# Attention kernel for one core: projections in column tiles and halves, VectorE work without the shared port, an early key tile, another output order

## Chip, cores and metric

One core of one Trainium2 chip. The metric is the device time of one execution in microseconds (us).

Engine names as the profile has them: PE is TensorE, PEld its weight load, ACT is ScalarE, DVE is VectorE, POOL is GpSimd, SP issues most DMAs. A line such as L1701 is a line of the kernel in question, so the same operation has other line numbers in other kernels.

## The reference, cut to what matters

```python
# S = 2048, D = 512, H = 32 heads of 16
def _A_ref(x, wq, wk, wv, wo):              # one key and value head for all query heads
    q = (x @ wq).reshape(B, S, H, 16).transpose(0, 2, 1, 3)
    k, v = x @ wk, x @ wv
    p = softmax(einsum("bhqd,bkd->bhqk", q, k) * 0.25)
    return heads_joined(einsum("bhqk,bkd->bhqd", p, v)) @ wo
def _B_ref(x, wqkv, w_phi, wo):             # linear attention
    q, k, v = ...                           # x @ wqkv
    pq, pk = q @ w_phi, k @ w_phi           # per head
    phi = lambda t: concat([softmax(t), softmax(-t)])
    kv, z = phi(pk)^T @ v, sum(phi(pk))
    return heads_joined((phi(pq) @ kv) / (phi(pq) @ z + 1e-6)) @ wo
return concat([_A_ref(...), _B_ref(...)], axis=-1)
```

Part A needs 32 x 2048 x 2048 exponentials, 2048 score tiles of 128x512. Part B is small.

## The kernel before

Half of the work is a Python list scheduler that runs while the program is built. Each piece of work is a job with an engine, an estimated length, predecessors and a priority; the scheduler keeps a model clock for every engine, and its order becomes the fixed order of each engine's instructions. A score tile's exponential goes to ACT (two tiles to one instruction, `f_PT`) or to DVE, which makes the bits of the result as an int16 (`f_Z`); POOL then shifts the bits of four such tiles at a time, three times, by integer additions, and each of the four versions has its own value product. Which tiles go where is decided as the model clock runs, so **any edit moves the split between ACT and DVE**.

```python
LOCK = ("dS", "qw")        # DVE jobs that must not run beside a POOL instruction
NEAR = 0.15                # us: a POOL addition due this soon goes ahead of such a job
T_B = (54.0, 600.0)        # when part B is released

def run(self):             # one round of the list scheduler
    ...
            t = max(r, self.pe_from(j, te) if eng == "pe" else te)
            j.asked = t
            if eng == "pool" or j.name[0] in self.LOCK:
                t = max(t, self.te_port)        # the port that DVE and POOL share is free
    ...
    s, j = min(picks, key=lambda p: (p[0], p[1].asked))
    if j.eng == "dve" and j.name[0] in self.LOCK:
        s, j = next((p for p in picks if p[1].eng == "pool" and p[1].asked <= s + self.NEAR
                     and self.te_port <= s + self.NEAR), (s, j))
    ...
def issue(self, j, start):
    ...
    if j.eng == "pool" or j.name[0] in self.LOCK:
        self.te_port = start + dur

def b_projv(self, st):     # one of six projections: four full-array matmuls in one piece
    for dc in range(4):
        mm = pe.matmul(ps[:, bank, :], lhsT=xT[:, dc, st*128:(st+1)*128], rhs=w[:, dc, :],
                       start=(dc == 0), stop=(dc == 3))
def b_bm(self, st):        # running sum of the softmax sums, 16 times
    v.tensor_tensor(out=bmx, in0=ssum[:, r, :], in1=bmx, op=ALU.add)
def b_vr(self, st):        # reciprocal, cast to bf16, 16 times
    v.tensor_copy(out=self.vS[:, r, :, :, 16:17], in_=rs.unsqueeze(3))

def finish_last(self):     # the tail: last denominator, then four output tiles of part A
    for i in (2, 3, 0, 1):
        ...                # products whose terms are there; 2 and 3 take all of them here
    for h in range(2):     # halves of the last denominator, shuffled to all partitions
        v.stream_shuffle(lnd[:, c], ps[:, ACC, c], [16] * 32)
    ...                    # 1/x = exp(-ln x) on ACT, multiplication, last products
    for i in (2, 0, 3, 1):
        eng = "act" if i > 1 else "dve"         # 0 and 1 add a partial product made before
        ...
        q.dma_start(out[0, (12+i)*128:(13+i)*128, 0:512], oa[:, i, :])   # queue: act if i > 1 else sp
```

Of the kernel before, what the change touches and what calls it, by code (L numbers as in the profile page):

```python
# [1160 lines left out]
class _Fast:  # L1161
# [15 lines left out]
    def __init__(self, nc, st, ins, out):  # L1177
# [24 lines left out]
        self.bmx = sb("bmx", [128, 64], F32)  # L1202
# [20 lines left out]
        self.ssum = sb("ssum", [128, 2, 64], F32)  # L1223
# [18 lines left out]
        self.free = [4, 5, 6, 7]  # L1242
        self.rec = None
# [10 lines left out]
        self.beside = False  # L1254
# [33 lines left out]
    def job(self, name, eng, dur, fn, after=(), mode=None, nb=0, frees=(), rel=0.0, prio=5.0, ok=None):  # L1288
        j = _Job(name, eng, dur, fn, after, mode, nb, frees, rel, prio, ok)
        j.left = {a for a in j.left if a not in self.issued}  # L1290
        self.njobs += 1
        j.seq = self.njobs
        for a in j.left:
            self.waiting.setdefault(a, []).append(j)
        if not j.left:
            self.cand[eng].append(j)
        return j

    def ready(self, j):
# [6 lines left out]
        t = j.rel  # L1306
# [11 lines left out]
        if nb:  # L1318
            fr = sorted(max(self.tr.get(("PS", b), (0.0,))[0], 0.0) + self.SEM for b in self.free)
            if len(fr) < nb:  # L1320
                return None
            t = max(t, fr[nb - 1])
        return t

    def issue(self, j, start):
# [11 lines left out]
        if j.eng == "pe":  # L1337
            self.beside = j.name[0] == "dq"
# [5 lines left out]
        if j.nb:  # L1344
            bs = sorted(self.free, key=lambda b: (self.tr.get(("PS", b), (0.0,))[0], b))[:j.nb]
            for b in bs:
                self.free.remove(b)
            self.bk[j.name] = bs
            self.held += j.name[0] != "dq"
        acc = self.acc_of(j)  # L1350
        if acc:
            self.bk[acc] = [min(self.free, key=lambda b: (self.tr.get(("PS", b), (0.0,))[0], b))]
# [75 lines left out]
    def head(self):  # L1428
# [27 lines left out]
        add("pool", lambda g: g.memset(self.bmx, 0.0), writes=["bmx"])  # L1456
# [31 lines left out]
        for k, t in (("wk_rep", 2.0), ("half1", 1.0), ("wv", 6.5), (("wq", 0), 3.5), (("wq", 1), 6.0), ("VA1", 3.0), ("ones", 1.0), ("zero", 1.0), ("bmx", 14.0), (("step", 0), 8.0), (("step", 1), 8.0)):  # L1488
            self.tw[k] = (t, "sp")
# [10 lines left out]
    def jobs_a(self):  # L1500
        ps, xT, job = self.ps, self.xT, self.job
        for kc in range(4):
            u = 0 if kc == 0 else 2
            job(("pk", kc), "pe", 0.86, (lambda kc: (lambda: self.proj_k(kc)))(kc), mode="full", nb=1, prio=u)
# [3 lines left out]
            job(("aK", kc), "dve", 0.60, (lambda kc: (lambda: self.absmax(self.KR[:, 0, kc * 512:kc * 512 + 512], kc, [("KR", 0, kc)])))(kc), after=[("KR", 0, kc)] + [("qa", 0)] * (kc == 0), prio=6)  # L1508
            job(("pva", kc), "pe", 0.42, (lambda kc: (lambda: self.proj_va(kc)))(kc), after=[("pq", 0), ("pk", kc)], mode="full", nb=1, prio=u + 0.5)
            job(("va", kc), "dve", 0.65, (lambda kc: (lambda: self.proj_va2(kc)))(kc), after=[("pva", kc)], frees=[("pva", kc)], prio=u + 0.5)  # L1510
        for ch in range(16):
            job(("pq", ch), "pe", 0.86, (lambda ch: (lambda: self.proj_q(ch)))(ch), mode="full", nb=1, prio=0 if ch == 0 else 2.2,
                ok=(lambda ch: (lambda: ch < 1 or (self.asc >= 2 * ch - 3 and (ch < 3 or self.qleft[2 * ch - 6] + self.qleft[2 * ch - 5] == 0))))(ch),
                after=[("pq", ch - 1)] if ch else [])
            job(("qa", ch), "dve", 0.60, (lambda ch: (lambda: self.proj_q2(ch)))(ch), after=[("pq", ch)], frees=[("pq", ch)], prio=1)
            job(("aq", ch), "dve", 0.60, (lambda ch: (lambda: self.absmax(self.QA[:, ch % 3, :], 4 + ch, [("QA", ch % 3)])))(ch), after=[("qa", ch)], prio=6)
        for qt in range(12):
            job(("op", qt), "pe", 0.86, (lambda qt: (lambda: self.outproj(qt)))(qt), mode="full", nb=1, prio=3.0, after=[("on", qt // 4 * 8 + a) for a in range(8)])
# [10 lines left out]
    def proj_k(self, kc):  # L1529
        ps, xT = self.ps, self.xT  # L1530
        bank = self.bank(("pk", kc))

        def fn(pe):
            mm = None
            for dc in range(4):
                mm = pe.matmul(ps[:, bank, :], lhsT=self.wk_rep[:, dc, :], rhs=xT[:, dc, kc * 512:(kc + 1) * 512], start=(dc == 0), stop=(dc == 3))
            return mm
        self.add("pe", fn, reads=[("AxT", kc), "wk_rep"], writes=[("PS", bank)])

    def proj_k2(self, kc, e):  # L1540

        ps, bank, half = self.ps, self.bank(("pk", kc)), self.half
        dst = self.KR[:, e, kc * 512:(kc + 1) * 512]
        self.add("dve", lambda v: v.tensor_scalar(out=dst, in0=ps[:, bank, :], scalar1=half[:, e:e + 1], scalar2=None, op0=ALU.mult),
                 reads=[("PS", bank), "half1"] + [("half", g) for g in range(4)], writes=[("KR", e, kc)])

# [26 lines left out]
    def proj_q(self, ch):  # L1573
# [3 lines left out]
        bank = self.bank(("pq", ch))  # L1577

        def fn(pe):
            mm = None  # L1580
            for dc in range(4):
                mm = pe.matmul(ps[:, bank, :], lhsT=self.wq[:, dc, A * 128:A * 128 + 128], rhs=xT[:, dc, qc * 512:(qc + 1) * 512], start=(dc == 0), stop=(dc == 3))  # L1582
            return mm
        self.add("pe", fn, reads=[("AxT", qc), ("wq", min(A, 1))], writes=[("PS", bank)])

    def proj_q2(self, ch):
        self.copy(self.QA[:, ch % 3, :], self.ps[:, self.bank(("pq", ch)), :], [("PS", self.bank(("pq", ch)))], [("QA", ch % 3)])
# [21 lines left out]
    def next_qk(self, i):  # L1609
# [6 lines left out]
        if not us:  # L1616
# [4 lines left out]
        self.job(("qk", i), "pe", 0.218, lambda: self.qk(us, b0), mode="row", prio=0, after=[("qa", sc // 2) for sc in {u[0] for u in us}] +  # L1621
                 [("KR", sc, k) for sc, k in {(u[0] % 2, u[1] // 4) for u in us}] + ([("qk", i - 1)] if i else []))
# [5 lines left out]
    def qk(self, us, b0):  # L1628
        reads = set()
        for sc, kap, g in us:  # L1630
            reads |= {("QA", sc // 2 % 3), ("KR", sc % 2, kap // 4)}
# [76 lines left out]
    def dq_ok(self):  # L1708
        if self.dbusy > self.DBUSY or self.dz_out >= self.NOUT:
            return False  # L1710
        if self.mode != "row" or self.beside:
# [777 lines left out]
```

## Time and profile before

| | before |
|---|---|
| time, median of 3 runs | 713.73 us (712.76 to 714.05) |
| span of the profiled run | 711.0 us |
| ACT exponentials / DVE tiles | 700 / 648 |
| head, ACT's stretch, tail | 9.25, 685.9, 15.8 us |

The output multiplications of part A on DVE, by line (shortest, median and longest in ns, then the start of the first and the last):

```profile
L1879 DVE TENSOR_TENSOR f_On<-f_accS,f_denS x16: 677/912/1375, 53.8 to 696.0; 128x512 bf16<-128x512 f32 x16
L1879 DVE TENSOR_TENSOR f_Ot<-f_accS,f_denS x15: 681/693/1207, 74.1 to 674.0; 128x512 bf16<-128x512 f32 x15
```

Both inputs lie in SBUF, and the same work takes 0.68 or 1.4 us. POOL's additions, from the costliest groups (busy us, mean ns, idle time before them and what ended it):

```profile
L1782 POOL INT64_ADD f_Z<-f_Z x486 | 512.7, 1055 | 167.5 <-DVE f_Z L1752 128.1
```

POOL is busy for 512.7 of 711.0 us. Of the 31 multiplications 16 take over 0.75 us, and each of these 16 overlaps a POOL instruction in the trace; 12 of the other 15 overlap one too and are not stretched. And the end of the tail, from the timeline (start, us, engine, line):

```profile
700.56 0.44 DVE L1942 STREAM_SHUFFLE f_ET<-f_ps 128x256 f32<-128x256 f32 x1
...
703.74 0.97 SPq L1961 DMA_DIRECT2D out_dram<-f_outA  x2
704.22 0.39 ACTq L1961 DMA_DIRECT2D out_dram<-f_outA  x1
...
705.29 1.12 ACTq L1961 DMA_DIRECT2D out_dram<-f_outA  x1
```

The four output tiles are issued between 703.74 and 705.29 and land, by the trace's DMA records, at 707.20, 707.51, 707.84 and 708.14. Then 2.9 us of fixed ending follow.

### The profile page before, as it was taken

Reading aid. Unit: us, or ns where it says so; the run is one execution under the profiler, and the core shown is the slowest. Engines: PE = TensorE matmul, PEld = TensorE weight load, DVE = VectorE, ACT = ScalarE, POOL = GpSimd, SP = SyncE. Lnnn points to the kernel's source line nnn. Section 1 sums busy time; section 2 is a strip of 40 time slices with the busy share of each in tenths; the row PEclk is TensorE's granted clock in tenths of the full one; section 3 lists DMA queues with packets and bytes.
Section 4 is the critical chain, followed back from the end, with each engine's and each line's share of the span. In section 5 each row is a group of like instructions: output and inputs, shape, how many; then the busy total and the mean of one; then the engine's idle time right before and its main releaser. Section 6 shows DMA issues by size and latency. Waiting matters only on the chain.

```text
span 711.0 us, 18172 instructions
## 1 busy us (share of the span) xinstructions
PE 669.8 (94%) x7493; PEld 211.0 (30%) x7548; DVE 620.6 (87%) x1039; ACT 683.7 (96%) x771; POOL 521.8 (73%) x522
## 2 busy tenths in 40 slices
PE   8999999999999999999999999999999999999995
PEld 3222223222323223332222322323332323333322
DVE  4789899998999999999788987889878989989974
ACT  5999999999999999999999999999999999999992
POOL 4488877777778667876878777678878787787870
PEclk9999999999999999999999999999999999999998
DMA  6611233110112110111110111111111210111212
GB/s 136 134 16 29 41 38 80 8 10 7 9 13 38 11 12 5 12 9 13 9 8 15 17 19 17 16 16 23 21 16 10 27 24 20 17 14 16 32 16 53
DMA packets 47890, 18.28 MB, mean 26 GB/s; under 512 B 38708, under 2 KB 45940, under 8 KB 47800
## 3 DMA queue, kind: packets, MB, share of 16 engines
q1 hardware_dynamic: 45400, 16.23, 18.0%
q8 instruction: 60, 0.98, 0.6%
q10 hardware_dynamic: 2400, 0.82, 0.5%
q14 instruction: 30, 0.25, 0.1%
HBM read 2.28 MB, written 4.19 MB: 9 GB/s over the span
## 4 chain that ended last, share of the span: by engine, by line
ACT 47%; PE 30%; DVE 20%; issue 1%; DMA 1%; POOL 1%; ACTq 0%; DVEq 0%
ACT f_PT L1647 45%; DVE f_Z L1752 11%; PE f_ps L1592 10%; PE f_ps L1812 8%; PE f_ps L1694 4%; PE f_ps L2246 2%; DVE f_ssum L2070 1%; DVE f_vS L2104 1%; ACT f_ET L2161 1%; PE f_ps L1582 1%; PE f_ps L1898 1%; DVE f_Wk L2216 1%; DMA f_AxT<-in_A_x_dram 1%; PE f_ps L2056 1%; DVE f_On L1879 1%
## 5 line engine op out<-in xcount | busy, mean ns | idle before, releaser
L1647 ACT ACTIVATE f_PT<-f_ps 128x1024 bf16<-128x1024 f32 x700 | 654.5, 1093 | 12.4 <-PE f_ps L1592 9.8
L1782 POOL INT64_ADD f_Z<-f_Z x486 | 512.7, 1055 | 167.5 <-DVE f_Z L1752 128.1
L1752 DVE TENSOR_SCALAR f_Z<-f_ps 128x512 int16<-128x512 f32 x648 | 426.0, 683 | 52.7 <-PE f_ps L1592 50.1
L1592 PE MATMUL f_ps<-f_QA,f_KR 32*128 32x512 bf16 x2048 | 280.2, 385 | 14.9 <-ACT f_PT L1647 11.3
L1812 PE MATMUL f_ps<-f_Z,f_VK 128*32 128x512 f16 x2592 | 227.5, 386 | 4.2 <-DVE f_Z L1752 1.6
L1592 PEld LDWEIGHTS f_ps<-f_QA,f_KR 32*128 32x128 bf16 x2048 | 70.4, 91 | 254.4 <-ACT f_PT L1647 224.8
L1694 PE MATMUL f_ps<-f_PT,f_VA 128*32 128x512 bf16 x1400 | 131.6, 385 | 0.1
L1812 PEld LDWEIGHTS f_ps<-f_Z,f_VK 128*32 128x32 bf16 x2592 | 56.4, 94 | 105.4 <-issue 61.2
L1694 PEld LDWEIGHTS f_ps<-f_PT,f_VA 128*32 128x32 bf16 x1400 | 33.6, 94 | 47.8 <-issue 44.7
L2216 DVE TENSOR_TENSOR f_Wk<-f_ps,f_wq 128x512 bf16<-128x512 f32 x32 | 21.9, 683 | 3.6 <-PE f_ps L2205 3.6
L1413 PE MATMUL f_ps<-f_ones,f_zero 128*128 128x512 bf16 (+4 forms) x112 | 20.2, 364 | 1.3 <-POOL f_zero L1432 1.3
L1419 DVE COPY f_accS<-f_ps 128x512 f32<-128x512 f32 x31 | 21.1, 680 | 0.0
L2104 DVE TENSOR_TENSOR f_vS<-f_ps,f_rs 128x1024 bf16<-128x1024 f32 x16 | 19.7, 1229 | 0.2 <-PE f_ps L2094 0.2
L2070 DVE TENSOR_REDUCE f_ssum<-f_Ek 128x64 f32<-128x1024 bf16 x16 | 19.3, 1205 | 0.0
L2161 ACT ACTIVATE f_ET<-f_ps 128x512 bf16<-128x512 f32 x32 | 18.8, 689 | 0.1
L2064 ACT ACTIVATE f_Ek<-f_ps 128x512 bf16<-128x512 f32 x32 | 18.2, 655 | 0.0
L1419 DVE CAST f_outB<-f_ps 128x512 bf16<-128x512 f32 x16 | 10.9, 683 | 6.7 <-PE f_ps L2246 6.7
L2154 PE MATMUL f_ps<-f_BxT,f_Wq 128*128 128x512 bf16 x56 | 14.8, 381 | 1.9 <-issue 1.0
L2246 PE MATMUL f_ps<-f_Bwo,f_oT 128*128 128x512 bf16 x57 | 15.0, 381 | 1.5 <-issue 1.0
L2094 PE MATMUL f_ps<-f_Bwv,f_BxT 128*128 128x512 bf16 x56 | 15.0, 381 | 1.2 <-DVE f_Z L1752 0.8
L1879 DVE TENSOR_TENSOR f_On<-f_accS,f_denS 128x512 bf16<-128x512 f32 x16 | 15.3, 958 | 0.8 <-DMA f_denS<-f_denS 0.8
L2056 PE MATMUL f_ps<-f_Wk,f_BxT 128*128 128x512 bf16 x53 | 14.1, 380 | 1.8 <-issue 1.5
(95 smaller groups left out, 281.7 us busy)
## 6 DMA issues: line engine op xcount, KB each, us to landing
f_denS<-f_denS SPq DMA_DIRECT2D x124, 30.0 KB, 3.1
out_dram<-f_outB SPq DMA_DIRECT2D x16, 128.0 KB, 1.8
f_denC<-f_accS SPq DMA_DIRECT2D x124, 2.0 KB, 1.7
f_denS<-f_denC SPq DMA_DIRECT2D x124, 2.0 KB, 1.7
out_dram<-f_outA SPq DMA_DIRECT2D x14, 128.0 KB, 2.8
f_On<-f_Ot SPq DMA_DIRECT2D x60, 16.0 KB, 1.8
f_Bwv<-in_B_wqkv_dram SPq DMA_DIRECT2D x1, 512.0 KB, 4.2
f_Bwo<-in_B_wo_dram SPq DMA_DIRECT2D x1, 512.0 KB, 4.5
```

The source lines that it names most:

```text
L1419: self.add("dve", lambda v: v.tensor_copy(out=out, in_=in_), reads=reads, writes=writes)
L1592: return pe.matmul(self.ps[:, bank, :], lhsT=self.KR[32 * g:32 * g + 32, sc % 2, kap * 128:(kap + 1) * 128], rhs=self.QA[32 * g:32 * g + 3 ...
L1647: self.add("act", lambda a: a.activation(out=PT[:, sl[0]:sl[0] + size, :], in_=ps[:, b0:b0 + size, :], func=ACT.Exp), reads=[("PS", b0 + i ...
L1694: mm = pe.matmul(ps[32 * g:32 * g + 32, bank, :], lhsT=VA[:, kap, :], rhs=PT[:, slots[g], :], start=start, stop=stop, tile_position=(0, 32 ...
L1752: self.add("dve", lambda v: v.tensor_scalar(out=o, in0=ps[:, bank, :], scalar1=self.Z1, scalar2=self.Z0, op0=ALU.mult, op1=ALU.add), reads ...
L1782: fn = lambda g: g.int64_add(out=b, in0=a, in1=256 * t * 0x1000100010001)
L1812: mm = pe.matmul(ps[32 * g:32 * g + 32, bank, :], lhsT=self.VK[:, t, kap, :], rhs=Zf[:, sl[g], :], start=start, stop=stop, tile_position=( ...
L2070: self.add("dve", lambda v: v.tensor_reduce(out=ssum[:, r, :], in_=Ek[:, r].rearrange("p a h f -> p (a h) f"), axis=AX.X, op=ALU.add), rea ...
L2104: self.add("dve", lambda v: v.tensor_tensor(out=vS[:, :, :, 0:16], in0=v3, in1=rs.unsqueeze(3).to_broadcast([128, 2, 32, 16]), op=ALU.mult ...
L2161: self.add("act", lambda e: e.activation(out=self.ET[:, sl, :], in_=self.ps[:, bank, :], func=ACT.Exp, scale=1.0 - 2.0 * a), reads=[("PS", ...
L2216: self.add("dve", lambda v: v.tensor_tensor(out=o, in0=i, in1=w.unsqueeze(3).to_broadcast([128, 2, 16, 16]), op=ALU.mult), reads=[("PS", b ...
L2246: mm = pe.matmul(ps[:, bank, :], lhsT=oT[:, r, C, :], rhs=self.Bwo[:, C, :], start=(C == 0), stop=(C == 3))
```

## The change

Its intent: (1) cut each projection in two halves of the contraction, in column tiles, so that TensorE can go back to scores between them; (2) take the small DVE instructions off the port that DVE and POOL share, and have the planner keep the larger ones away from POOL's additions; (3) start the first exponential earlier from 128 keys and two query halves; (4) finish the output tiles of the tail in the order in which they are done. Many constants of the scheduler move too. The core, cuts marked:

```diff
 def job(self, name, eng, dur, fn, ...):
+    if nb and name[0] in self.SPLIT and dur > 0.8:      # two jobs, each half of the contraction
+        first = (name[0] + "0",) + name[1:]
+        self.job(first, eng, dur / 2, self.of_part(fn, 0), after, mode, nb, (), rel, prio, ok)
+        return self.job(name, eng, dur / 2, self.of_part(fn, 1), [first], mode, 0, frees, 0.0, self.SECOND)
 ...
 def b_projv(self, st):                                  # the same in five other projections
-    for dc in range(4):
-        mm = pe.matmul(ps[:, bank, :], lhsT=xT[:, dc, st*128:(st+1)*128], rhs=w[:, dc, :], start=(dc == 0), stop=(dc == 3))
+    for dc in terms:                                    # 0, 1 or 2, 3
+        for g in range(4):
+            mm = pe.matmul(ps[32*g:32*g+32, bank, :], lhsT=xT[:, dc, st*128+32*g:st*128+32*g+32], rhs=w[:, dc, :], start=(dc == 0), stop=(dc == 3), tile_position=(0, 32*g))
 ...
 def b_bm(self, st):                                     # now for every fourth st
-    v.tensor_tensor(out=bmx, in0=ssum[:, r, :], in1=bmx, op=ALU.add)
+    v.tensor_reduce(out=ssum[:, o, :], in_=ssum[:, k:k+5, :].rearrange("p k f -> p f k"), axis=AX.X, op=ALU.add)
 def b_vr(self, st):
-    v.tensor_copy(out=self.vS[:, r, :, :, 16:17], in_=rs.unsqueeze(3))
+    v.tensor_reduce(out=self.vS[:, r, :, :, 16], in_=rs.unsqueeze(3), axis=AX.X, op=ALU.max)
 ...
+    job(("pk", -1), "pe", 0.22, lambda: self.proj_k(-1), mode="full", prio=-3)    # 128 keys
+    job(("ph", 0), "pe", 0.43, lambda: self.proj_q(0, 1), ...)                    # second query half
+    job(("qh", 0), "act", 0.28, lambda: self.proj_q2(0, 1), ...)                  # its copy on ACT
 ...
 def finish_last(self):
-    for i in (2, 3, 0, 1):
+    for i in (0, 2, 1, 3):
 ...
-    for i in (2, 0, 3, 1):
+    for i in range(4):                                  # even tiles on ACT, odd ones on DVE
 ...
-    q.dma_start(...)  # queue="act" if i > 1 else "sp"
+    q.dma_start(...)  # after all copies; queue="act" if i == 2 else "sp"
 ...
-    LOCK = ("dS", "qw")
+    LOCK = ("dS", "qw", "on", "kvfin")   # on: output multiplications; kvfin: end of the key-value sums
+    SPLIT = ('bk', 'bv', 'bq', 'pq', 'op', 's8')
-    PLEFT = 8.0;  QS = 0.9;  ZLOW = 4;  LEFT = 8;  AGE = 3.0;  AGED = 0.8;  DBUSY = 3.0;  T_B = (54.0, 600.0)
+    PLEFT = 20.0; QS = 0.5;  ZLOW = 3;  LEFT = 16; AGE = 2.0;  AGED = 0.6;  DBUSY = 5.0;  T_B = (43.0, 620.0)
```

## The prediction

> **What bounds the kernel now.** I read the page's busy shares first, then the costliest groups, then what ScalarE (ACT) waits for, and last the timelines of the two ends.
>
> ```profile
> PE 669.8 (94%) x7493; PEld 211.0 (30%) x7548; DVE 620.6 (87%) x1039; ACT 683.7 (96%) x771; POOL 521.8 (73%) x522
> ...
> L1647 ACT ACTIVATE f_PT<-f_ps 128x1024 bf16<-128x1024 f32 x700 | 654.5, 1093 | 12.4 <-PE f_ps L1592 9.8
> L1752 DVE TENSOR_SCALAR f_Z<-f_ps 128x512 int16<-128x512 f32 x648 | 426.0, 683 | 52.7 <-PE f_ps L1592 50.1
> ```
>
> ACT is busy 683.7 of 711.0 us. There are 2048 attention tiles of 128x512: 1400 get their exponential on ACT, two to an instruction (x700), and 648 on VectorE (DVE). Inside its stretch ACT hardly rests:
>
> ```profile
> core 0: us, PE busy (x) PEld busy (x) DVE busy (x) ACT busy (x) POOL busy (x), PEclk, DMA share, GB/s
> 9.25:695.20 685.95, 654.43 (x7416) 205.15 (x7473) 613.01 (x1025) 679.63 (x764) 514.90 (x497) 1.00 0.18 23
> 0.00:9.25 9.25, 7.79 (x32) 2.89 (x33) 1.94 (x3) 1.29 (x2) 6.59 (x25) 1.00 0.73 159
> 695.20:711.10 15.90, 7.56 (x53) 2.97 (x46) 5.62 (x12) 2.75 (x6) 0.26 (x1) 0.81 0.17 55
> ```
>
> So the time is three pieces: a head of 9.25 us before the first exponential, an ACT stretch of 685.9 us, a tail of 15.8 us after the last one. The stretch can be split further. ACT instructions overlap, so the cost of one more is the distance of their ends, not the mean of 1093 ns. The chain of waits, in a stretch where ACT led, has these lines:
>
> ```profile
> 357.25 0.98 ACT f_ET L2161 x2
> 358.23 15.59 ACT f_PT L1647 x17
> ```
>
> 15.59 / 17 = 0.917 us each; other unbroken runs give the same, and I take 0.916. The 64 other activations (keys and queries of part B) cost 0.98 / 2 = 0.49 each. The stretch without any loss would be 1.05 (one full length) + 699 x 0.916 + 64 x 0.49 = 672.7 us. It is 685.9, so **13.2 us are lost**, though the wait list shows only 6 us of idle time there: a delay shorter than the overlap of two activations shows as a longer record, not as idleness. Going through the ends of successive activations I find some 75 late ones. About 48 of them (5.7 us) have a projection on TensorE (PE) between the two score groups before them, mostly by 50 to 120 ns; the other two dozen (about 7 us) are few and large, where PE had waited for DVE or sat behind a queue of value products.
>
> DVE is made late by stretched instructions:
>
> ```profile
> L2080 DVE TENSOR_TENSOR f_bmx<-f_ssum,f_bmx x16: 217/256/1172, 92.2 to 319.8; 128x64 f32<-128x64 f32 x16
> L2085 DVE CAST f_vS<-f_rs x16: 295/380/1022, 92.0 to 320.5; 128x64 bf16<-128x64 f32 x16
> ...
> L1752 DVE TENSOR_SCALAR f_Z<-f_ps x648: 622/683/721, 23.6 to 688.0; 128x512 int16<-128x512 f32 x162
> ```
>
> The columns are shortest/median/longest in ns. The same tiny instruction takes 217 or 1172 ns, while the bit-trick exponential, which reads PSUM, never moves by more than 100 ns. GpSimd (POOL) additions of 1055 ns run most of the time.
>
> **What the Trainium skill says.** "SBUF — State Buffer", Who interferes with whom: VectorE and GpSimd share a port pair under an exclusive lock held for a whole instruction; a cast or copy in a two-port mode, or a two-input operation with both inputs in SBUF against a GpSimd read, contends; `tensor_reduce` on trn2 never does. The trace agrees: the two lines above are exactly these two kinds, the longest exceed the shortest by 955 and 727 ns, about one POOL addition, and the reductions over the exponentials stay within 1160 to 1212 ns. "TensorEngine Tiling (Array Packing)", Key Properties: "Changing tiling mode (not just tile) drains the TensorE"; tiles work in parallel. The trace has both: sixteen 32-column value products take 0.98 us, the same as four full projections (0.97), and there is about 0.1 us between a row-tiled score group and what follows it.
>
> **The change, part by part.** The changed program is a static order that a list scheduler made, so I count its instructions.
>
> 1. *Split between the engines.* 710 exponentials on ACT for 700, 628 tiles on DVE for 648. ACT: +10 x 0.916 = +9.2 us, wholly on the path. This is the main cost.
>
> 2. *Projections.* Each was four full-array matmuls in one piece (0.86 us and two mode changes). Now each is two halves of 8 column-tile matmuls, 0.43 us, in the mode of the value products. The multiplications cost no less; what changes is the block that stands between two score groups. Weighing the printed order with 0.213 us a full matmul or four column tiles and 0.11 a mode change, blocks of over 0.9 us fall from 108 to 36; the number of mode changes hardly moves (1455 to 1470). ACT holds two score buffers, so a block that fits into about 0.9 us costs it nothing. Of the 5.7 us beside projections I expect 4 to 4.5 back.
>
> 3. *Port lock on DVE.* The running sum becomes 4 reductions of 320 elements (about 0.4 us each, by the 0.41 us of other 256-element instructions) for 16 additions of 7.6 us in sum; the casts become reductions of about 0.2 us, 3.2 for 7.5 us. The output multiplications (31, 677 to 1375 ns, 7.4 us above their floor of 0.68) stay, but the planner now keeps them off POOL's additions. With 20 x 0.657 = 13.1 us less of bit tricks, DVE loses some 6 + 4.3 + 5 + 13.1 = 28 us: 620.6 to about 592. DVE has slack, so none of this is direct gain; it takes away surprises that made PE late. Of the other 7 us lost I expect 4 to 4.5 back.
>
> Together the loss goes from 13.2 to about 4.5 us, a gain of 8.7.
>
> 4. *Early keys (head).* Before, keys of 512 columns, queries, the query copy and the score group run in series:
>
> ```profile
> 6.13 1.02 PE L1536 MATMUL f_ps<-f_AxT,f_wk_rep 128*128 128x512 bf16 x4
> 7.00 1.89 PE L1582 MATMUL f_ps<-f_AxT,f_wq 128*128 128x512 bf16 x8
> 7.20 0.75 DVE L1544 TENSOR_SCALAR f_KR<-f_ps,f_half 128x512 bf16<-128x512 f32 x1 [7.20 <-PE f_ps L1536]
> 8.06 0.69 DVE L1419 CAST f_QA<-f_ps 128x512 bf16<-128x512 f32 x1
> ```
>
> Now 128 key columns come first (0.22 us instead of 0.86), the queries in two halves of 256 columns (0.92 together), whose copies run on DVE (0.41) and on ACT (0.4). From the landing at 6.1: 6.35 keys, 7.4 the second half, about 8.0 its copy on ACT, scores at 8.1, first exponential at about 8.5. Gain 0.75 us.
>
> 5. *Tail.* Before, from the last exponential's end (695.18) to the first shuffle of the last tile (700.53) there are 5.35 us, filled by the last of part B; from there to the end 10.5. The new order has finished part B by then, but the last partial output product comes after the last value product and seven fillers. It needs a multiplication on DVE and a copy by DMA whose queue first sends the broadcast of the previous denominator. Reckoning from that reciprocal as in the old trace (686.10 to 695.97 until its result is used) it starts about 2.2 us after the last exponential; 6 matmuls (1.3) and its copy (0.7 and waits) follow, so the shuffle comes at about 4.6. The output tiles then finish as they are done: the second ACT copy need no longer wait behind a DMA issue (0.47 us idle in the old trace), worth about 0.85. Tail: 4.6 + 9.65 = 14.2 for 15.8, gain 1.6.
>
> Sum: +9.2 - 8.7 - 0.75 - 1.6 = -1.85 us, and +0.3 for the small ACT copy in the head's account is already in it. Span 711.0 to about 709.1; the run times lie 2.7 above the span (713.73 - 711.0): about **711.5**.
>
> **Rivals.** *The loss stays at 13.* If delays really come from PE being nearly full (94%) and not from long blocks or DVE, the ten exponentials are paid in full: 713.7 + 9.2 - 2.3 = about 720.5. For it: PE's number of mode changes is the same. Against: late exponentials cluster beside projections, and PE gets 20 bit-trick tiles' worth (80 value products, 4.3 us) less work by moving 20 tiles to ACT, less 1.1 for their ACT value products. *The halves starve DVE.* A split projection holds one of the four free PSUM banks longer; DVE's bit tricks already wait 50.1 us for scores. The in-order PE would then wait for DVE more often: loss 20, 727. The lower count of DVE tiles speaks for some of it, but the planner has already priced that in. *Everything fits*: loss 0 to 1, giving 707. That is the floor, since ten more exponentials cannot be hidden on an engine that is 99% busy in its stretch. *Tail copy late*: the partial product depends on four DMA issues and a landing; 2 us more would make it 713.5.
>
> **Range and chances.** The loss term carries the uncertainty: 0 to 10 us gives 707 to 717. A gain of over 2% would need 14.3 us, 5 more than even no loss, with these head and tail, can give; 2% slower would need a loss above 23. Central value 711.5, range 706.5 to 717.5; chances 0.02, 0.94, 0.04.
>
> **What would show it.** Right: 710 ACT exponentials at 0.916 us end to end; ACT's stretch near 686.5 us with fewer late ones beside projections; the running sum and cast lines flat in time; DVE near 592 us busy; first exponential at 8.5; the shuffle 4.6 us after the last exponential. Wrong, if the late exponentials are as many and as large as before, if PE waits for DVE more, if the output multiplications are still stretched, or if column-tile halves take more than 0.43 us.

## The result, and the profile after

| | before | after |
|---|---|---|
| time, median of 4 runs | 713.57 us (712.76 to 714.05) | 715.08 us (714.71 to 715.25) |
| ratio, 95% interval | | 1.0022 (1.0004 to 1.0039) |

A ratio is the mean time of one kernel's fast runs over that of the other's of the same rounds, so not quite the ratio of the medians quoted. The time is the same within 2%, 0.2% longer.

The changed kernel's busy shares and costliest groups, from its page:

```profile
PE 682.2 (96%) x8606; PEld 206.8 (29%) x8609; DVE 602.3 (84%) x1009; ACT 689.2 (97%) x782; POOL 498.4 (70%) x507
...
L1701 ACT ACTIVATE f_PT<-f_ps 128x1024 bf16<-128x1024 f32 x710 | 661.8, 1122 | 4.2 <-PE f_ps L1748 2.3
L1836 POOL INT64_ADD f_Z<-f_Z x471 | 489.1, 1038 | 192.2 <-DVE f_Z L1806 153.3
L1806 DVE TENSOR_SCALAR f_Z<-f_ps 128x512 int16<-128x512 f32 x628 | 417.9, 684 | 74.1 <-PE f_ps L1646 69.7
```

DVE has 18.3 us less to do, ACT ten exponentials more, and POOL idles longer before its additions (192.2 for 167.5 us). The stretch of ACT, the head and the tail, from the windows (columns as in the prediction):

```profile
8.78:697.00 688.22, 667.92 (x8520) 201.38 (x8518) 595.86 (x995) 684.73 (x774) 491.84 (x484) 1.00 0.19 24
0.00:8.78 8.78, 7.13 (x60) 3.06 (x64) 1.31 (x4) 1.67 (x2) 6.28 (x23) 1.00 0.75 145
697.00:713.00 16.00, 7.15 (x30) 2.41 (x31) 5.16 (x11) 2.76 (x7) 0.26 (x1) 0.85 0.14 42
```

The account is made as in the prediction: base = 1.05 + (exponentials - 1) x 0.916 + 64 x 0.49; lost = stretch minus base. (The tail starts at the end of the last exponential, 697.01.)

| us | exponentials | head | base | lost | tail | span |
|---|---|---|---|---|---|---|
| before | 700 | 9.25 | 672.7 | 13.2 | 15.84 | 711.0 |
| predicted | 710 | 8.5 | 681.9 | 4.5 | 14.2 | 709.1 |
| after | 710 | 8.78 | 681.9 | 6.4 | 15.95 | 713.0 |

So the loss was more than halved, 6.8 us, and the ten exponentials took it back with 2.4 us on top (9.2). The head gave 0.5; the tail gave nothing. Of the late exponentials (more than 50 ns behind the pace) some 24 are left of some 75; those beside a projection fell from about 48 (5.7 us) to 5 to 7 (0.8 us). What ACT still waits for:

```profile
ACT f_PT L1701 <- PE f_ps L1748: 2.3, 2, 2.2
...
ACT f_PT L1701 <- PE f_ps L1646: 1.5, 4, 0.7
```

The columns are us in total, times, longest. One single wait of 2.2 us, at 604, makes a third of the loss; it ended with a value product (L1748), which made room in the ring of exponential results.

On DVE, the lines that answer to the stretched ones:

```profile
L1933 DVE TENSOR_TENSOR f_On<-f_accS,f_denS x16: 673/682/990, 83.9 to 697.9; 128x512 bf16<-128x512 f32 x16
L1933 DVE TENSOR_TENSOR f_Ot<-f_accS,f_denS x15: 680/682/1306, 85.7 to 689.9; 128x512 bf16<-128x512 f32 x15
...
L2144 DVE TENSOR_REDUCE f_ssum<-f_ssum x4: 691/710/714, 136.5 to 325.3; 128x64 f32<-128x320 f32 x4
...
L2150 DVE TENSOR_REDUCE f_vS<-f_rs x16: 407/420/451, 88.5 to 321.8; 128x64 bf16<-128x64 f32 x16
```

The median multiplication is at its floor now (sum of the 31: 22.4 us for 28.5). The reductions are flat in time, as hoped, but slower at their floor than predicted: 0.71 us for 0.4, and 0.42 us for 0.2, where the cast's shortest was 0.295. The casts' 7.5 us became 6.8: hardly a saving.

The head, from the timeline:

```profile
7.71 0.38 ACT L1637 ACTIVATE f_QA<-f_ps 128x256 bf16<-128x256 f32 x1 [4.62 <-PE f_ps L1628]
...
8.35 0.40 PE L1646 MATMUL f_ps<-f_QA,f_KR 32*128 32x512 bf16 x4
```

The query copy starts 0.1 us later than reckoned and 0.26 us lie between its end and the scores.

The tail, from the chain of waits (start, us, what), with the lines between left out:

```profile
689.17 2.72 DMA f_denS<-f_denC
...
691.91 0.88 SPq L1909
...
695.35 0.56 SPq L1939
...
697.32 2.64 DMA f_On<-f_Ot
...
700.27 0.61 PE f_ps L1975 x2
...
702.44 0.46 DVE f_ET L1999
```

This one queue decides the tail. The copy of an output multiplication (L1939) could be issued only after the reciprocal of the next denominator had landed (691.89) and its broadcast had been issued (four issues of some 0.8 us); it landed at 699.96, 2.9 us after the last exponential, and only then could the partial output product (L1975) begin. Its multiplication itself was ready long before, from the timeline:

```profile
689.89 0.68 DVE L1933 TENSOR_TENSOR f_Ot<-f_accS,f_denS 128x512 bf16<-128x512 f32 x1
```

The broadcast that it needs had landed at 682.02 by the DMA records: it ran 7.9 us later, being on the new protected list, with POOL busy. And the outputs:

```profile
705.35 1.45 SPq L2019 DMA_DIRECT2D out_dram<-f_outA  x3
706.11 0.37 ACTq L2019 DMA_DIRECT2D out_dram<-f_outA  x1
```

The last one is issued at 706.46, 4.0 us after the shuffle instead of 4.7 before; but they land at 709.06, 709.39, 709.71 and 710.02, again a third of a microsecond apart, the last 7.6 us after the shuffle as before. The earlier issue was lost in the landing.

### The profile page after: what moved, and what is told of

Same layout as the page of the kernel before. It is cut to its first block, busy times and chain, and to the rows that moved or that the text cites. A ratio compares the mean times of both kernels' runs of the same rounds, so it can differ in the third digit from the quotient of the medians.

```text
span 713.0 us, 20307 instructions
## 1 busy us (share of the span) xinstructions
PE 682.2 (96%) x8606; PEld 206.8 (29%) x8609; DVE 602.3 (84%) x1009; ACT 689.2 (97%) x782; POOL 498.4 (70%) x507
## 4 chain that ended last, share of the span: by engine, by line
ACT 58%; PE 33%; DVE 3%; DMA 2%; POOL 1%; SPq 1%; issue 1%; DVEq 0%; POOLq 0%
ACT f_PT L1701 55%; PE f_ps L1646 12%; PE f_ps L1866 9%; PE f_ps L1748 5%; ACT f_Ek L2127 2%; DVE f_Z L1806 2%; PE f_ps L1955 2%; PE f_ps L2319 1%; ACT f_ET L2231 1%; POOL f_Z L1836 1%; PE f_ps L2225 1%; PE f_ps L2275 1%; PE f_ps L2300 1%; DMA f_AxT<-in_A_x_dram 1%; PE f_ps L1628 1%
## 5 line engine op out<-in xcount | busy, mean ns | idle before, releaser
L1701 ACT ACTIVATE f_PT<-f_ps 128x1024 bf16<-128x1024 f32 x710 | 661.8, 1122 | 4.2 <-PE f_ps L1748 2.3
L1836 POOL INT64_ADD f_Z<-f_Z x471 | 489.1, 1038 | 192.2 <-DVE f_Z L1806 153.3
L1806 DVE TENSOR_SCALAR f_Z<-f_ps 128x512 int16<-128x512 f32 x628 | 417.9, 684 | 74.1 <-PE f_ps L1646 69.7
L1866 PE MATMUL f_ps<-f_Z,f_VK 128*32 128x512 f16 x2512 | 216.8, 385 | 4.9 <-PE f_ps L1866 1.8
L1748 PE MATMUL f_ps<-f_PT,f_VA 128*32 128x512 bf16 x1420 | 133.0, 385 | 0.1
L1748 PEld LDWEIGHTS f_ps<-f_PT,f_VA 128*32 128x32 bf16 x1420 | 34.1, 94 | 50.6 <-issue 45.2
L1443 PE MATMUL f_ps<-f_ones,f_zero 128*128 128x512 bf16 (+6 forms) x109 | 21.2, 365 | 1.5 <-POOL f_zero L1462 1.3
L2172 DVE TENSOR_TENSOR f_vS<-f_ps,f_rs 128x1024 bf16<-128x1024 f32 x16 | 21.1, 1320 | 0.1
L2162 PE MATMUL f_ps<-f_Bwv,f_BxT 128*32 128x512 bf16 x256 | 19.6, 383 | 0.3
L2225 PE MATMUL f_ps<-f_BxT,f_Wq 128*32 128x512 bf16 x256 | 19.6, 383 | 0.2
L1628 PE MATMUL f_ps<-f_AxT,f_wq 128*32 128x512 bf16 (+1 forms) x272 | 19.5, 371 | 0.3
L2319 PE MATMUL f_ps<-f_Bwo,f_oT 128*32 128x512 bf16 x256 | 19.6, 382 | 0.1
L2119 PE MATMUL f_ps<-f_Wk,f_BxT 128*32 128x512 bf16 x256 | 19.6, 383 | 0.0
```

What stands on the lines that cost most here:

```text
L1628: mm = pe.matmul(ps[32 * g:32 * g + 32, bank, a:a + n], lhsT=self.wq[:, dc, A * 128 + 32 * g:A * 128 + 32 * g + 32], rhs=xT[:, dc, qc * 51 ...
L1701: self.add("act", lambda a: a.activation(out=PT[:, sl[0]:sl[0] + size, :], in_=ps[:, b0:b0 + size, :], func=ACT.Exp), reads=[("PS", b0 + i ...
L1748: mm = pe.matmul(ps[32 * g:32 * g + 32, bank, :], lhsT=VA[:, kap, :], rhs=PT[:, slots[g], :], start=start, stop=stop, tile_position=(0, 32 ...
L1806: self.add("dve", lambda v: v.tensor_scalar(out=o, in0=ps[:, bank, :], scalar1=self.Z1, scalar2=self.Z0, op0=ALU.mult, op1=ALU.add), reads ...
L1836: fn = lambda g: g.int64_add(out=b, in0=a, in1=256 * t * 0x1000100010001)
L1866: mm = pe.matmul(ps[32 * g:32 * g + 32, bank, :], lhsT=self.VK[:, t, kap, :], rhs=Zf[:, sl[g], :], start=start, stop=stop, tile_position=( ...
```

## The experiments

Twelve kernels, all correct, each timed in rounds with the kernel before on the same chip: e1 to e4 together (before 712.22 us), e5 to e8 (713.35), e9 to e11 (713.59), e12 alone (713.89). Since the scheduler answers every edit, each has its own number of exponentials; the accounts of all are in this table, and the time lost is compared, not only the time.

| | exponentials | head | lost | tail | span | time, median | ratio to before (95%) |
|---|---|---|---|---|---|---|---|
| after | 710 | 8.78 | 6.4 | 15.95 | 713.0 | 715.08 | 1.0022 (1.0004 to 1.0039) |
| e1_nolock | 700 | 8.69 | 18.2 | 16.85 | 716.4 | 719.67 | 1.0112 (1.0095 to 1.0128) |
| e2_nosplit | 706 | 8.77 | 13.2 | 15.91 | 716.1 | 716.63 | 1.0063 (1.0034 to 1.0092) |
| e3_full | 708 | 9.21 | 19.1 | 24.49 | 732.8 | 734.49 | 1.0322 (1.0300 to 1.0344) |
| e4_beforelock | 706 | 9.75 | 17.5 | 37.46 | 740.9 | 742.00 | 1.0412 (1.0395 to 1.0430) |
| e5_onpool | 702 | 8.54 | 397.5 | 19.28 | 1099.9 | 1101.82 | 1.5440 (1.5368 to 1.5512) |
| e6_tail | 710 | 8.84 | 6.2 | 12.45 | 709.3 | 710.96 | 0.9967 (0.9951 to 0.9984) |
| e7_copies | 710 | 9.22 | 14.0 | 15.95 | 721.0 | 720.41 | 1.0094 (1.0078 to 1.0111) |
| e8_full2 | 710 | 8.66 | 10.4 | 13.66 | 714.6 | 717.30 | 1.0054 (1.0028 to 1.0080) |
| e9_near | 702 | 8.90 | 9.5 | 12.43 | 705.3 | 706.25 | 0.9886 (0.9865 to 0.9906) |
| e10_yield | 700 | 8.89 | 7.5 | 11.35 | 700.4 | 702.24 | 0.9841 (0.9824 to 0.9858) |
| e11_oldtail | 710 | 8.84 | 6.4 | 16.10 | 713.2 | 715.07 | 1.0024 (1.0007 to 1.0041) |
| e12_nolock2 | 702 | 9.14 | 13.2 | 10.94 | 707.8 | 708.67 | 0.9922 (0.9906 to 0.9939) |

(In e4 four of the 64 other activations come after the last exponential, so its base counts 60.) Each account is that of the one profiled run, and the spans of one kernel's runs differ by up to some 4 us (11 in e5).

One part of the column "lost" needs care. In seven of these profiles (e1, e2, e3, e4, e7, e9 and e12) the granted TensorE clock is 0.50 for one to three stretches of 3.4 to 10.2 us in the middle of the run, and e5 has many of them; in before, after, e6, e8, e10 and e11 it is 1.00 from 10 us on to 690 us. Two stretches of e7, from its windows (the clock is the third number from the end):

```profile
334.90:338.20 3.30, 3.30 (x30) 0.65 (x26) 2.10 (x4) 2.44 (x3) 2.08 (x2) 0.50 0.00 0
638.70:642.00 3.30, 3.30 (x29) 0.49 (x22) 2.36 (x4) 2.59 (x3) 2.99 (x3) 0.50 0.05 7
```

TensorE is busy through both, and exponentials there come up to 1.51 us apart instead of 0.916. The lateness of the exponentials that end in such a stretch, or within 1 us after it, sums to 2.9 us in e1, 3.5 in e2, 8.0 in e3, 6.9 in e4, 4.1 in e7, 2.5 in e9 and 2.6 in e12. That is about the most that the clock can have cost there, for some of these delays had begun before it fell. Not every run of a kernel is hit alike: the four runs of e7 have spans of 717.4 us (mean clock 0.996) to 721.0 us (0.993, the profiled one). All but one of the stretches in the seven begin within 2.5 us after a pause of TensorE of 0.4 us or more (1.95 us in e1, 1.88 in e7), but other such pauses, one of 1.71 us in e3 among them, are followed by none; what brings them on is not shown. Where a comparison hangs on it, the loss outside these stretches is given too.

My theory going in was that the ten extra exponentials were the price of the longer protected list, and that the list was not worth it. For it stood the planner's own counts: over 36 variants of part B's release times, the median plan has 698 exponentials on ACT for the kernel before and 706 with the longer list alone, 712 for the changed kernel and 702 without the longer list. These are my counts of built programs, and no times.

### e1_nolock: the changed kernel without the longer list

```diff
-    LOCK = ("dS", "qw", "on", "kvfin")
+    LOCK = ("dS", "qw")
```

> The changed kernel with the planner's lock list put back to its old two entries, so that the 31 output multiplications and the finish of the key-value sums are again placed without regard to GpSimd. The built program has 700 exponentials on ScalarE and 648 tiles on VectorE, as the kernel before, for 710 and 628. Theory A (the lock list is what moved ten exponentials to ScalarE and delayed the multiplication of tile 29 to the tail): head 8.8, 672.7 us without loss, loss 6 to 9, tail about 14.7: span about 704, time about 706, some 9 us faster than the changed kernel. Rival B (the lock earns its price, stretched multiplications bring the lost time on ScalarE back to the 13 us of before): span 710, time 712.7, within 3 us of the changed kernel. In both, the multiplications are stretched again, up to 1.3 us.

Measured: 700 exponentials, as the theory said, but 18.2 us lost for 6.4, more than the 13 of rival B too, and 719.67 us. **The theory fell**: protection costs 9.2 us of exponentials and is worth 11.8 us of loss here, or 8.9 us outside the half-clock stretch. So in this pair the list about pays for itself; it does not cost the 9 us that the theory gave it. The multiplications stretch again, 31.4 us in sum:

```profile
L1933 DVE TENSOR_TENSOR f_On<-f_accS,f_denS x16: 681/1130/1466, 54.3 to 697.7; 128x512 bf16<-128x512 f32 x16
L1933 DVE TENSOR_TENSOR f_Ot<-f_accS,f_denS x15: 681/925/1484, 72.8 to 678.2; 128x512 bf16<-128x512 f32 x15
```

And one place shows how a stretched DVE instruction can reach ACT, though DVE is no bound. From its timeline, the finish of the key-value sums:

```profile
330.35 1.32 DVE L2207 TENSOR_TENSOR f_KVn<-f_kvS,f_mask 128x128 bf16<-128x128 f32 x2
...
332.06 3.08 DVE L1806 TENSOR_SCALAR f_Z<-f_ps 128x512 int16<-128x512 f32 x5
...
332.80 0.38 PE L1646 MATMUL f_ps<-f_QA,f_KR 32*128 32x512 bf16 x1 [1.95 <-DVE f_Z L1806]
...
334.31 1.02 ACT L1701 ACTIVATE f_PT<-f_ps 128x1024 bf16<-128x1024 f32 x1 [2.11 <-PE f_ps L1646]
```

Two of its multiplications take 1.32 us together, where two take 0.55 in the changed kernel (274 to 277 ns each); the bit tricks start late; TensorE, in order, stands 1.95 us at a score tile for DVE; ACT then stands 2.11 us. The half-clock stretch begins at 333.6 us, after TensorE's wait and before ACT's end, so a part of the 2.11 us may be the clock's.

### e2_nosplit: column tiles, but each projection in one piece

```diff
-    SPLIT = ('bk', 'bv', 'bq', 'pq', 'op', 's8')
+    SPLIT = ()
```

> The changed kernel with each projection's sixteen column-tile matmuls in one piece instead of two halves; 706 exponentials on ScalarE. Theory A (short blocks between score groups are what took away the delays beside projections): loss on ScalarE rises from 6.3 to 10 or 11, with about 40 late exponentials beside projections again; minus 3.7 us for four exponentials less: time 715 to 716, same as the changed kernel. Rival (column tiles alone do it, because they need no mode change next to the value products): loss stays at 6, time about 711.5.

Measured: 13.2 us lost for 6.4 in the profiled run, which was the second longest of four (715.15 to 719.24). 36 late exponentials beside projections again (3.5 us) for 5 to 7 (0.8 us). Two half-clock stretches hold up to 3.5 us of the 13.2; the other 9.7 are near the theory's 10 or 11. The split does what it was made for; by the times, with four exponentials fewer, leaving it out costs 0.4%.

### e3_full and e8_full2: full-array projections

```diff
-    SPLIT = ('bk', 'bv', 'bq', 'pq', 'op', 's8')
+    SPLIT = ()
 # and in the six projections, 15 of the 16 query tiles among them:
-                for g in range(4):
-                    mm = pe.matmul(ps[32*g:32*g+32, bank, :], ..., tile_position=(0, 32*g))
+                mm = pe.matmul(ps[:, bank, :], ...)          # and mode="full"
 # e8_full2 has also
-    T_B = (43.0, 620.0)
+    T_B = (48.0, 600.0)
```

> The changed kernel with the projections as four full-array matmuls in one piece, as before the change (only the first query tile keeps its early halves); 708 exponentials on ScalarE. Theory A: loss 10 to 12 us for 6.3, minus 1.8 for two exponentials: time 717 to 719. Rival (the form of the projections does not matter, the reduced delays come from VectorE alone): loss stays at 6, time about 713.5.

> Like e3_full (projections as four full-array matmuls in one piece), but part B is planned from 48 to 600, which the planner ends as early as that of the changed kernel; 710 exponentials. Theory A (whole projections delay scores): the long tail of e3_full goes (24.5 to about 16), the loss stays high, 12 to 18 us for 6.3: span 719 to 725. Rival (e3_full was slow because its part B came late, the form of the projections hardly matters): loss 6 to 9, time 715 to 718.

e3 missed both of its expectations: 734.49 us, 19.1 us lost. It is no clean test: with these release times its plan left so much of part B to the end that the tail was 24.5 us, and two half-clock stretches hold up to 8.0 us of the loss. e8 releases part B so that the tail (13.66) is in order. Measured in e8: 10.4 us lost for 6.4, with 39 late exponentials beside projections (4.5 us). There is no half-clock stretch in it. The loss lies between the two expectations (12 to 18, 6 to 9), and the time, 717.30 us, in the rival's range. Against the prediction the size fits, 4 to 4.5 us: column tiles in halves are worth about 4 us of loss in this plan. The spans of e8's four runs go from 713.0 to 716.5 us, so this is good to some 2 us, and part B's release differs between the two. Column tiles alone don't do it, for e2 has them in one piece and loses about as much as e8 does. Halves of full-array matmuls were not tried, so what is shown is the halving, and not that it needs column tiles.

### e4_beforelock: the kernel before with the longer list alone

```diff
-    LOCK = ("dS", "qw")
+    LOCK = ("dS", "qw", "on", "kvfin")
 # and the guard of the changed kernel for where a flag is loaded
```

> The kernel before with the new lock list alone (and the guard that places the read of the flag late enough); 706 exponentials on ScalarE for 700. Theory A (the lock list by itself costs): six exponentials more, 5.5 us, less what the unstretched multiplications save of the loss, perhaps 3: time 715 to 718. Rival B (the lock earns its price): loss falls from 13 to 7 or less, time 711 to 713.

Measured: 742 us, with a tail of 37.5 us; part B came late, and four of its activations run after the last exponential. Both expectations missed. This tells nothing clean about the list alone; it tells only that with the constants of before this list gave a bad plan.

### e5_onpool: the output multiplications on POOL

```diff
-            job(("on", sc), "dve", 0.60, ..., prio=1.3,
+            job(("on", sc), "pool", 1.3, ..., prio=0,
-        self.add("dve", lambda v: v.tensor_tensor(out=o, in0=accS[:, r, :], in1=R[:, r, :], op=ALU.mult),
+        self.add("pool", lambda v: v.tensor_tensor(out=o, in0=accS[:, r, :], in1=R[:, r, :], op=ALU.mult),
-    LOCK = ("dS", "qw", "on", "kvfin")
+    LOCK = ("dS", "qw", "kvfin")        # AGED = 0.8, T_B = (39.0, 600.0), the flag read at sp=(11, 4)
```

> The changed kernel with the 31 output multiplications moved from VectorE to GpSimd, so that they need no lock and can stretch nothing on VectorE; part B starts at 39 and ends at 600 in the planner's scale, ageing 0.8. 702 exponentials on ScalarE. GpSimd's time for 512 fp32 elements with two inputs is not in any trace yet; the plan assumes 1.3 us. If it is near that: head 8.8, 674.6 us without loss, loss 5 to 7, tail about 15: span 704, time about 706.5, faster than both kernels. Rival: the multiplication on GpSimd takes 2 us or more, its integer additions come late, TensorE waits for them, loss 12 or more: time 713 or above.

A plain miss: 1101.82 us at a granted clock of 0.81. The multiplication itself takes 1254 ns on POOL, but its groups show what was not reckoned with:

```profile
L1836 POOL INT64_ADD f_Z<-f_Z x483 | 501.9, 1039 | 315.7 <-issue 178.2 <-DVE f_Z L1806 95.1 <-POOL f_Z L1836 12.2
L1933 POOL TENSOR_TENSOR f_On<-f_accS,f_denS 128x512 bf16<-128x512 f32 x16 | 20.1, 1254 | 112.0 <-issue 112.0
```

Before each of the 31 multiplications POOL stands 7.0 us (112.0 / 16), and before the next addition, 30 times, 5.9 us (178.2 / 30), waiting for nothing that the profile shows, beside records of a change of POOL's configuration. Together that is 397 us, as much as the whole loss of 397.5; what the low clock took of it was not separated.

### e6_tail: two edits for the tail

```diff
-    LAST = dict(..., sp=(12, 4))
+    LAST = dict(..., sp=(15, 4))        # the flag is read earlier in the DMA queue's order
-                        if eng == "pool" or j.name[0] in self.LOCK:
+                        if eng == "pool" or (j.name[0] in self.LOCK and j.name != ("on", 29)):
```

> The changed kernel with the tail mended in two lines: the multiplication of tile 29 is not held back by the lock, so its copy by DMA goes ahead of the broadcast for tile 30, and SyncE reads the flag before those transfers and not between them. 710 exponentials, order up to the last 20 us as in the changed kernel. Theory (the tail lost what its split gained to these two waits on the DMA queue): shuffle 1.5 us after the last exponential instead of 5.4, tail 12 for 15.9, loss 6.3 unchanged: span 709, time 711. Rival (the tail is set by the landing of the output or of the broadcast for tile 30): tail above 14.5, time 714 or more.

Multiplication 29 no longer waits for the port, so its copy is issued ahead of the broadcast; and the flag no longer stands between two transfers of a reciprocal. Measured: 710.96 us; head and loss the same (6.2), tail 12.45 for 15.95, and from the last exponential to the shuffle 2.08 us instead of 5.43. So 3.5 us of the tail were the order of that queue. The two edits were not tried apart.

### e7_copies: the small DVE instructions as before

```diff
-        v.tensor_reduce(out=ssum[:, o, :], in_=ssum[:, k:k + 5, :]..., op=ALU.add)     # 4 times
+        v.tensor_tensor(out=bmx, in0=ssum[:, r, :], in1=bmx, op=ALU.add)               # 16 times
-        v.tensor_reduce(out=self.vS[:, r, :, :, 16], in_=rs.unsqueeze(3), axis=AX.X, op=ALU.max)
+        v.tensor_copy(out=self.vS[:, r, :, :, 16:17], in_=rs.unsqueeze(3))
```

> The changed kernel with the running sum (16 additions) and the reciprocal casts as they were before; 710 exponentials as in the changed kernel. Theory (port locks that the planner does not know make VectorE late and cost ScalarE): these instructions stretch up to 1 us again, loss rises from 6.3 to 9 to 11 us, time 717.5 to 720. Rival (VectorE has slack enough here): loss within 1.5 us of 6.3, time 715.

Measured: 720.41 us, the same 710 exponentials, 14.0 us lost for 6.4, in the longest of its four runs. Two half-clock stretches hold up to 4.1 us of this, which leaves 9.9; the run with the shortest span is 3.6 us shorter. So the small instructions are worth some 3.5 to 4 us of loss, inside the theory's 9 to 11 us, and not the 7.6 of the profiled run. By line:

```profile
L2143 DVE TENSOR_TENSOR f_bmx<-f_ssum,f_bmx x16: 163/464/944, 93.1 to 321.9; 128x64 f32<-128x64 f32 x16
...
L2148 DVE CAST f_vS<-f_rs x16: 309/408/1099, 89.0 to 320.8; 128x64 bf16<-128x64 f32 x16
```

16.6 us in sum, for 9.6 as reductions, though DVE has slack. The planner believed 0.13 us and the chip took up to 1.1; that this surprise makes the loss, by the way that e1's timeline shows at one place, is the likely reading, though this plan's order differs elsewhere too. The multiplications at the end of the key-value sums, though on the protected list, take up to 1121 ns here at 327 to 332 us (274 to 277 in the changed kernel); TensorE's pause of 1.88 us and the first half-clock stretch follow them. Its head is 0.44 us longer too; why is not known.

### e9_near and e10_yield: protection kept, additions no longer let ahead

```diff
 # both on top of e6_tail; e9_near (sp=(13, 4)):
-    NEAR = 0.15
+    NEAR = 0.05
 # e10_yield (sp=(12, 4)):
-    NEAR = 0.15
-    T_B = (43.0, 620.0)
+    NEAR = -1.0
+    T_B = (43.0, 590.0)
```

> e6_tail with one number of the planner changed: a locked VectorE instruction lets GpSimd go first only if GpSimd would start within 0.05 us, instead of 0.15 (and the flag read kept off the last transfers). The lock list stays. 702 exponentials on ScalarE for 710. Theory (the lock cost ten exponentials only because GpSimd always went first and the locked multiplications waited, holding back accumulators; the protection itself is free): multiplications as unstretched as in e6_tail, loss 6 to 8, head 8.8, 674.5 without loss, tail 12.5: span 702.5, time 704.5. Rival (GpSimd now comes late and TensorE waits for its products): loss 14, time 711, as e6_tail.

> e6_tail with the locked VectorE instructions always going before GpSimd, and part B planned to end at 590 instead of 620. 700 exponentials on ScalarE. Theory: loss 5 to 8, 672.7 without loss, head 8.8, tail 12: span 700, time 702, the fastest so far. Rival: as for e9_near, loss 14, time 709.

If protection is worth its price, perhaps the price is in how it is kept: with NEAR = 0.15 a protected multiplication steps back each time an addition is nearly due. Measured: e9 702 exponentials, loss 9.5 us, 706.25 us; e10 700 exponentials, loss 7.5 us, 702.24 us, as expected. e9's loss is above the 6 to 8 us expected, in the longest of its four runs; a half-clock stretch holds up to 2.5 us of it. The multiplications stay near their floor (21.4 and 22.2 us in sum; in e10 the medians are 682 ns).
POOL keeps its 486 additions and the split of the kernel before, from e10's groups:

```profile
L1836 POOL INT64_ADD f_Z<-f_Z x486 | 513.5, 1057 | 158.5 <-DVE f_Z L1806 117.9 <-POOL f_Z L1836 8.1 <-DVE f_mqk L2027 0.8
```

e10 beats both kernels: 1.6% less than before (0.9841), inside the 2% that count as the same but clear of the noise. Between e6 and e10 only constants of the scheduler changed: ten exponentials fewer for 1.3 us more loss, and a tail 1.1 us shorter.

### e11_oldtail: the output order of before

```diff
-        for i in (0, 2, 1, 3):                  # and the partial products for tiles 1 and 3
+        for i in (2, 3, 0, 1):                  # and those for tiles 0 and 1
-        for i in range(4): ...                  # one output DMA on ACT's queue, three on SP's
+        for i in (2, 0, 3, 1): ...              # two and two
```

> The changed kernel with the order of the last output products as it was before the change (tiles in halves of the array order, two outputs sent by ScalarE). Theory (the end is set by the landing of the four output transfers and not by when the last copy is issued, so the split by tile gained nothing): from the first shuffle to the end 10.5 us as in both kernels, within 0.25; time 715. Rival (the split did gain its 0.85 us and something else took it): 11.3 us, time 716.

Measured: 715.07 us, 0.01 apart from the changed kernel; from the shuffle to the end 10.17 us for 10.52, just outside the 0.25 that the theory allowed. The old order is if anything 0.35 us quicker there; the shuffle itself came 0.5 us later after the last exponential (5.93 us), behind a reciprocal that landed at 692.61 for 691.89. The new output order is worth nothing.

### e12_nolock2: the best version without the longer list

```diff
 # on top of e10_yield
-    LOCK = ("dS", "qw", "on", "kvfin")
+    LOCK = ("dS", "qw")
```

> This is the run with the eager yield and the mended tail (700 exponentials on ScalarE, 702.24 us), with the output multiplications and the finish of the key-value sums taken off the protected list; the plan has 702 exponentials, +1.8 us. Asked: was the loss of 18.2 us in the earlier run without protection the doing of the stretched multiplications, or luck of that one plan? Theory (protection is worth it): the 31 output multiplications again sum to some 28 to 32 us instead of 22.2, the loss in ScalarE's stretch is 12 to 19 us instead of 7.5, and the time is 709 to 716 us. Rival (luck of the plan): the multiplications stretch just as much, but the loss stays at 6 to 9 us and the time is 703 to 706 us; then protection is worth next to nothing and the saving lies with the order alone.

e1 was one plan of a scheduler that answers every edit, so this asks again with other release times. Measured: 702 exponentials, multiplications 31.1 us in sum, 13.2 us lost for 7.5, 708.67 us: in the span 7.4 us more than e10. The loss is inside the range that the theory gave, near its lower end, and the time just below its range, with a shorter tail (10.94 us). But a half-clock stretch holds up to 2.6 us of the loss, and two of e12's four runs, at a mean clock of 0.996, have spans of 705.8 us, 2.0 less than the profiled one. So protection is worth 3.1 to 5.7 us of loss in this pair and 8.9 to 11.8 in the other: the sign is the same in both, the size depends on the plan, and what the list brings in the end hangs on how many exponentials it costs.

## Why the prediction was right, and where not

The range held, but not the direction: 2.2 us faster was forecast, and the measured ratio is 1.0022, slower. 715.08 us lies 3.6 above the central value. Against the predicted span of 709.1 the measured 713.0 is 3.9 longer: tail +1.75, loss +1.9, head +0.3. All three missed to the same side, so no errors cancelled. Two sums on the range are slips that changed nothing: by its own terms a gain of 2% needs 7.5 us, not 5, more than no loss can give, and 2% slower needs a loss above 21 us, not 23. By its steps:

1. *Split between the engines*: right. +10 exponentials at 0.916 us were paid in full; the pace is unchanged. The prediction took the count from the built order and didn't ask what made it. The runs show that it was the way in which the protected list is kept: e9 keeps the list with 702, e10 with 700.

2. *Projections*: right in mechanism and size. Late exponentials beside projections went from 5.7 to 0.8 us (4 to 4.5 predicted back, 4.9 found), and e8, with full projections, loses 4.0 us more than the changed kernel. By e2 the halves do it, and not the column tiles as such.

3. *Port lock on DVE*: mechanism right, term mis-sized. From 13.2 us the loss fell to 6.4 and not to 4.5; the 1.9 us are less than one single wait of 2.2 us for a value product. The kernel before had one such wait, of 1.0 us, which the prediction didn't count apart. DVE's saving was 18.3 us and not 28, by these terms: the bit tricks gave 8.1 us instead of 13.1 (426.0 to 417.9 us busy; one takes 683 and 684 ns in the mean, so their records overlap less), the casts 0.8 instead of 4.3 and the running sum 4.8 instead of 6, since the reductions cost 0.42 and 0.71 us instead of 0.2 and 0.4; the multiplications gave 6.1, more than the 5 reckoned; and another line, the products of values and reciprocals, took 1.5 us more (19.7 to 21.1). Outside the half-clock stretches e7, with the small instructions as before, loses 3.5 us more, and e1 and e12, without the longer list, lose 8.9 and 3.1 us more than their partners (7.6, 11.8 and 5.7 as profiled).

4. *Early keys*: gain 0.47 us for 0.75, the scores 0.25 us later than reckoned.

5. *Tail*: **this step failed, in both halves.** "The shuffle comes at about 4.6" after the last exponential: it came at 5.43, since the copy by DMA was queued behind a broadcast and landed 2.9 us after the last exponential, and the product reckoned for 2.2 started at 3.3. The prediction had this as a rival and did not take it; it missed that the multiplication was held for 7.9 us, though its input lay ready. e6 undoes both, and the shuffle comes at 2.08. "Worth about 0.85": the issue of the last output did come 0.7 us sooner after the shuffle, but what ends the tail is the landing of four outputs one behind another, and this didn't move. e11 shows it: the old order gives the same time, and is no slower from the shuffle on.

Of the rivals, "the loss stays at 13" and "the halves starve DVE" are ruled out by the loss of 6.4; "tail copy late" (713.5) was the nearest to what happened.

What stays open: how much the list does in the kernel before by itself (e4 was spoilt by its late part B), what brings on the half-clock stretches, and whether the edits brought them; how the tighter yielding rule comes to ten exponentials fewer; that a multiplication that steps back again and again delays what hangs on it is argued, not shown. The early keys and the other constants of the scheduler that moved with the change were not tried by themselves.

## What to carry to other kernels

When an engine is full, count first what a change adds to it: 9.2 us of added work took back 6.8 us of removed delays, and the way to keep both gains was to find the rule of the planner that had moved the work. An instruction whose length depends on what runs beside it can hold up an in-order neighbour even from an engine with slack, as at one place in e1; the likely reason is that the order was made with the short length. Before a lost microsecond is put down to an edit, look at the granted clock in the stretch where it was lost: here that halved one difference (7.6 to 3.5 us in e7). In a tail, ask what the last transfer lands behind, not when it is issued.

## What the Trainium skill lacked or had wrong

- "GPSIMD Engine Reference", Instruction dispatch, has about 6 us (5.95 measured) for the first call to a freshly loaded kernel, "with no visible profile instruction". e5 has waits of that size at each of 31 changes from integer addition to TENSOR_TENSOR (7.0 us) and at each of 30 changes back (5.9 us), so an alternation of the two costs 12.9 us each time; that they are this load is not shown. The page doesn't say that the price comes back at every change.
- "SBUF — State Buffer", Who interferes with whom, has `tensor_reduce` as never contending. The runs agree: 407 to 451 ns in 16 instructions, where the cast had 295 to 1022. It doesn't say what the swap costs: at the floor the reduction of the same 64 elements takes 0.42 us for 0.295, and one of 320 elements 0.71 us.
- The same section tells who is blocked and for how long, not that a block on an engine with slack can reach another engine through a fixed order: 7 us more on DVE went with some 3.5 us more loss on ACT (e7, outside its half-clock stretches), though DVE is busy for only about 84% of the span. No page was found to have this.
- "TensorEngine Tiling (Array Packing)", Key Properties, has tiles in parallel and the drain at a change of mode. It has no advice on splitting a contraction so that other work can go between; here halves in column tiles were worth 4.0 us of loss against full projections in one piece (e8), and column tiles in one piece next to nothing (e2).
